# The last batch's token mixing as seven half products instead of eight, in a kernel whose matmul engine is always busy

## The chip, the cores and the metric

One core of a Trainium2 chip. The metric is the device time of one execution in microseconds (us), median of several. All data are float32. Engines: TensorE (PE, with its weight loads as PEld), VectorE (DVE), ScalarE (ACT), GpSimd (POOL), SyncE (SP, which issues all transfers).

## What is computed

Linear attention gives x, and a gated network with token mixing follows. Four batches, 1088 tokens, d_model 128, d_ff 1024; the mixing matrix is 1088 x 1088.

```python
def _moe_ref(x, w_in, w_spatial, b_spatial, w_out):
    h = np.maximum(x @ w_in, 0.0)
    u, v = h[..., :d_ff // 2], h[..., d_ff // 2:]
    v_n = (v - mean(v)) / np.sqrt(var(v) + 1e-06)          # over the 512 features
    v_s = np.einsum('ts,bsd->btd', w_spatial, v_n) + b_spatial[None, :, None]
    return (u * v_s) @ w_out
```

The product of `w_spatial` with `v_n` is the mixing; it is the largest part of the work.

## The kernel before

Every float32 operand of a matmul is kept as a high part, which the matmul takes exactly, and a low part (the rest); one product is three matmuls: high by high, low by high, high by low. `wTh` and `wTl` hold `w_spatial` transposed in SBUF for the whole kernel: 9 tiles of 128 source tokens (`kt`; the ninth holds the last 64 with the bias) by 1088 target tokens.

For each batch, `attention` makes x and then v (normalised on DVE), and `main` does the mixing. It runs over four blocks `d` of 128 features and three column groups `c` of target tokens (`CH`: 424, 332, 332 wide). For each of the 12 blocks, `hidden` makes u (three matmuls into PSUM bank `pu`, ReLU on ACT), `spatial` the mixing in one of two PSUM banks `sp`: for `kt` 0 to 7 three matmuls (L1018, L1020, L1027) and two for the ninth tile (L1018, L1029), 26 in all. `gate` then multiplies the bank by u on DVE (L1054), ACT casts the result to its high part (L525), DVE subtracts for the low part (L456), and `out_mm` adds its product with `w_out` (L446 to L448) to one of three `po` banks. A bank `sp` can be written anew only after the DVE's gate has read it. Line 936 and its neighbours split v into `vh` and `vl` for the next block.

What is executed when is not the order of the code: `Order.schedule` arranges the recorded operations on each engine from hand-set tables (`LEADS`, `T_MAIN`, `PACE`). Each engine then works strictly in the order it was given. Attention of the next batch is interleaved with the mixing of this one; in the last batch there is no next attention, and from about 260 us on PE has mixing, `hidden` and `out_mm` alone.

## Time and profile before

| | |
|---|---|
| time, median of 3 runs (lowest, highest) | 326.54 us (326.52, 327.94) |
| profiled execution, from first to last instruction | 325.6 us |
| PE busy | 319.2 us, 98% |
| DVE busy | 199.9 us, 61% |
| ACT busy | 150.9 us, 46% |
| POOL busy | 47.0 us, 14% |
| granted TensorE clock | 1.000 of full speed, 2.4 GHz, throughout |

The page states the span, 325.6 us, and no separate time for the profiled execution; the median lies 0.9 us above the span, which is taken as what lies around it. In the rows, DVE, ACT, POOL and PE are busy times of instructions; matmuls overlap, so a matmul's own duration (0.31 us) says less than the distance from one start to the next. A bracket at a row's end names the idle time before it and what ended it.

### The profile page before, as it was taken

The numbers are of one execution on the slowest core, as the hardware profiler recorded it, in microseconds if no ns is written. First come the engines' busy times: TensorE is split into PE (matmuls) and PEld (weight loads), VectorE is DVE, ScalarE is ACT, GpSimd is POOL, SyncE is SP. The second block draws the span as 40 slices with busy tenths as digits, with TensorE's granted clock in tenths as the row PEclk, the third lists the DMA queues.
The fourth block names the chain that finished last, engine by engine and source line by source line (L and its number), as shares of the span: only waits on it lengthen the run. The fifth ranks groups of instructions, "written<-read, shape, count | busy, mean of one in ns | idle before, by whom it ended". The sixth has DMA issues, their size and how long they took to land.

```text
span 325.6 us, 6652 instructions
## 1 busy us (share of the span) xinstructions
PE 319.2 (98%) x2655; PEld 303.7 (93%) x2655; DVE 199.9 (61%) x439; ACT 150.9 (46%) x357; POOL 47.0 (14%) x59
## 2 busy tenths in 40 slices
PE   8999999999999999999999999999999999999996
PEld 7877899999999899989999989999999999999995
DVE  4999899354599982679985899873222341022122
ACT  3389666634676464357542875642232242112211
POOL 1000001667300004350002812100000000000000
PEclk9999999999999999999999999999999999999999
DMA  6941059764011252310114410000000000000002
GB/s 206 337 146 49 22 148 300 231 193 128 0 48 44 84 162 89 117 34 24 45 45 129 142 50 21 0 2 0 2 0 1 29 21 23 0 0 2 0 0 70
DMA packets 18961, 23.97 MB, mean 74 GB/s; under 512 B 2546, under 2 KB 18674, under 8 KB 18930
## 3 DMA queue, kind: packets, MB, share of 16 engines
q1 hardware_dynamic: 18930, 23.54, 23.4%
q8 instruction: 21, 0.34, 0.4%
q14 instruction: 10, 0.08, 0.1%
HBM read 20.46 MB, written 3.06 MB: 72 GB/s over the span
## 4 chain that ended last, share of the span: by engine, by line
PE 83%; DMA 6%; SPq 3%; ACT 2%; POOL 2%; issue 2%; DVE 1%; POOLq 0%; ACTq 0%
PE sp L1018 18%; PE sp L1027 17%; PE sp L1020 16%; PE sd L446 3%; PE sd L447 3%; PE sd L448 3%; DMA pl<-abd 3%; PE po L446 2%; PE po L447 2%; PE po L448 2%; PE pu L446 2%; PE sp L1029 2%; PE pu L447 2%; PE pu L448 2%; DMA v<-in_vA 2%
## 5 line engine op out<-in xcount | busy, mean ns | idle before, releaser
L1018 PE MATMUL sp<-wT,vh 128*128 128x332 f32 (+1 forms) x414 | 133.8, 323 | 0.0
L1020 PE MATMUL sp<-wT,vl 128*128 128x332 f32 (+1 forms) x368 | 119.1, 324 | 0.3 <-DVE vl L965 0.3
L1027 PE MATMUL sp<-wT,vh 128*128 128x332 f32 (+1 forms) x368 | 116.9, 322 | 0.0
L1018 PEld LDWEIGHTS sp<-wT,vh 128*128 128x128 f32 x414 | 77.8, 188 | 1.9 <-ACT vh L962 0.3
L1020 PEld LDWEIGHTS sp<-wT,vl 128*128 128x128 f32 x368 | 69.1, 188 | 1.8 <-DVE vl L965 1.1
L1027 PEld LDWEIGHTS sp<-wT,vh 128*128 128x128 f32 x368 | 69.0, 188 | 0.4 <-DVE wT L573 0.2
L1054 DVE TENSOR_TENSOR u<-sp,u 128x332 f32<-128x332 f32 (+1 forms) x40 | 20.7, 517 | 51.7 <-PE sp L1029 42.7
L1010 ACT ACTIVATE u<-pu 128x332 f32<-128x332 f32 (+1 forms) x40 | 18.5, 463 | 36.9 <-PE pu L448 21.0
L456 DVE TENSOR_TENSOR g<-u,g 128x332 fp32r<-128x332 f32 (+1 forms) x38 | 21.8, 575 | 22.3 <-PE po L447 15.1
L525 ACT CAST g<-u 128x332 fp32r<-128x332 f32 (+1 forms) x38 | 18.1, 484 | 28.2 <-DVE u L1054 19.1
L874 DVE BATCH_NORM_STATS2 st<-vt 128x6 f32<-128x512 f32 x36 | 24.4, 688 | 8.2 <-ACT vt L872 7.9
L872 ACT ACTIVATE vt<-sd 128x512 f32<-128x512 f32 x36 | 21.7, 607 | 10.3 <-PE sd L448 9.5
L852 DVE RECIPROCAL c<-c 128x384 f32<-128x384 f32 (+1 forms) x9 | 21.8, 2418 | 6.7 <-ACT c L850 6.7
L791 POOL TENSOR_TENSOR pl<-pl,pl 128x384 f32<-128x384 f32 (+1 forms) x18 | 17.8, 1004 | 49.8 <-DMA pl<-abd 48.3
L934 ACT CAST vh<-vt 128x384 fp32r<-128x384 f32 x36 | 17.5, 513 | 11.6 <-PE sp L1018 6.8
L459 POOL TENSOR_TENSOR r<-pl,r 128x384 fp32r<-128x384 f32 (+1 forms) x18 | 17.3, 972 | 20.9 <-ACT r L525 15.4
L936 DVE TENSOR_TENSOR vl<-vt,vh 128x384 fp32r<-128x384 f32 (+1 forms) x36 | 19.2, 542 | 1.2 <-ACT vh L934 0.9
L573 POOL TENSOR_TENSOR wT<-pl,wT 128x332 fp32r<-128x332 f32 (+1 forms) x9 | 8.4, 956 | 56.7 <-ACT wT L570 55.0
L894 DVE TENSOR_SCALAR vt<-vt,mv,sm 128x512 f32<-128x512 f32 x33 | 16.3, 538 | 0.0
L446 PE MATMUL pu<-x,wih 128*128 128x332 f32 (+1 forms) x48 | 16.1, 335 | 0.0
L570 ACT CAST wT<-pl 128x332 fp32r<-128x332 f32 (+1 forms) x27 | 12.8, 503 | 6.7 <-DMA pl<-in_wT 6.7
L447 PE MATMUL pu<-x,wih 128*128 128x332 f32 (+1 forms) x48 | 15.7, 327 | 0.0
(153 smaller groups left out, 497.8 us busy)
## 6 DMA issues: line engine op xcount, KB each, us to landing
pl<-in_wT SPq DMA_DIRECT2D x18, 166.0 KB
v<-in_vA SPq DMA_DIRECT2D x12, 198.0 KB
kt<-in_kT SPq DMA_DIRECT2D x12, 192.0 KB
pl<-abd SPq DMA_DIRECT2D x12, 192.0 KB
pl<-abd SPq DMA_DIRECT2D x24, 96.0 KB
pl<-in_wT SPq DMA_DIRECT2D x9, 212.0 KB
c<-in_qT SPq DMA_DIRECT2D x7, 192.0 KB
out<-u SPq DMA_DIRECT2D x6, 166.0 KB
```

The costliest lines, as they stand in the source:

```text
L446: nc.tensor.matmul(o, ah, bh, start=start, stop=False)
L447: nc.tensor.matmul(o, ah, bl, start=False, stop=False)
L448: nc.tensor.matmul(o, al, bh, start=False, stop=stop)
L456: return lambda: nc.vector.tensor_tensor(out=o(), in0=a(), in1=bb(), op=ALU.subtract)
L852: op("DVE", 135 + 6.3 * n, lambda x32=x32, n=n: nc.vector.reciprocal(out=x32[:, :n], in_=x32[:, :n]), w=[x32])
L872: op("ACT", c_act(512, True) + 16, lambda pv=pv, t=t: nc.scalar.activation(vt[:, t], pv.ap, AF.Relu), r=[pv], w=[(vt, t)])
L874: op("DVE", 690, lambda stats=stats, t=t: nc.vector.bn_stats(out=stats.ap, in_=vt[:, t]), r=[(vt, t)], w=[stats])
L936: return lambda: eng.tensor_tensor(out=vl[:, kk:kk + n], in0=x()[:, :n], in1=vh[:, kk:kk + n].bitcast(F32), op=ALU.subtract)
L1018: nc.tensor.matmul(sp[:, :cw], vh[:, kt], wTh[:, kt, cs], start=(kt == 0), stop=False)
L1020: nc.tensor.matmul(sp[:, :cw], vl[:, kt], wTh[:, kt, cs], start=False, stop=False)
L1027: nc.tensor.matmul(sp[:, :cw], vh[:, kt], wTl[:, kt, cs], start=False, stop=False)
L1054: op("DVE", c_dve(cw), lambda: nc.vector.tensor_tensor(out=u.ap, in0=sp[:, :cw], in1=u.ap, op=ALU.mult), r=[sp], w=[u], lead=LEAD[1])
```

## The change

In batch 3 (`FAST`), `main_fast` takes the place of `main`. The first eight tiles of source tokens are cut into two halves of four, the target tokens into two halves of 552 columns (268 + 284; twelve columns between 756 and 768 of the padded matrix are a gap of zeros), and the feature blocks go in pairs (d, e). This makes a 2 x 2 by 2 x 2 block product, which Winograd's form of Strassen's method does with seven block products instead of eight, of sums of blocks. The ninth tile (`remainder`) stays apart.

- `weights_fast` loads 48 pieces of `w_spatial` again from HBM (128 x 268 or 284, 4 buffers `w`, issued after 185 us in the schedule's time), forms the sums S1, S2, S4 and S3 from them on DVE (72 operations) and splits them into high (32 casts on ACT) and low parts. They are written where attention's buffers lie, S3 over columns of `wT`.
- `prepare(p)` forms the sums of blocks of v for a pair.
- `product` does one block product (4 tiles x 3 matmuls for each of the two column pieces). What several results share is kept: `keep` copies a bank to SBUF on ACT, and `gate` with `other` first adds it (L1424) and then multiplies (L1434).
- `out_mm` adds up one pair at a time; the first pair's result is kept by an ACT copy, the second pair's added on DVE (L1472), and four stores leave instead of three.
- `CH`, `AT` and `PITCH` change the order and place of the column groups, and the tables of the schedule are new for batches 2 and 3.

```diff
-CH = [(0, 424), (424, 332), (756, 332)]
-AT = [0, 436, 820]
+CH = [(332, 424), (0, 332), (756, 332)]
+AT = [332, 0, 768]
+CW = (268, 284)
+FROM = ((0, 268), (548, 816))
+FAST = (3,)
+RELOAD = 185.0
+USE_POOL = False
-T_MAIN = (36.0, 126.0, 244.0, 299.0)
-PACE = (1.305, 0.8, 1.056, 1.506)
+T_MAIN = (36.0, 126.0, 222.612, 333.931)
+PACE = (1.305, 0.8, 1.0625, 1.8734)
...
+        def block(kt, half, c):
+            t = tl("w", f"wr{kt}{half}{c}", [P, CW[1]])
+            load(t, lambda: t[:, :CW[c]], wT[kt * P:(kt + 1) * P, c0:c0 + CW[c]], CW[c] // 2, after=RELOAD)
...
+        def halves(j, i, c, x):
+            op("ACT", c_act(n), lambda: nc.scalar.copy(out=hi(), in_=x[:, :n]), r=[x], w=wh)
+            both(c_dve(n), tt(lo, lambda: x[:, :n], lambda: hi().bitcast(F32), ALU.subtract), [x, *wh], wl, c_pool(n))
+        for i in range(4):
+            for c in range(2):
+                a21, a22 = block(i, 1, c), block(4 + i, 1, c)
+                sum_of(a22, a21, a22, ALU.add, c)
+                halves(1, i, c, a22)
...
+            a11, a12 = block(i, 0, c), block(4 + i, 0, c)
+            both(c_dve(n), tt(lambda: a11[:, :n], lambda: hi().bitcast(F32), lambda: a11[:, :n], ALU.subtract), wh, [a11], c_pool(n))
+            both(c_dve(n), tt(lambda: a11[:, :n], lambda: a11[:, :n], lambda: lo().bitcast(F32), ALU.add), wl, [a11], c_pool(n))
+            halves(2, i, c, a11)
+            sum_of(a12, a12, a11, ALU.subtract, c)
+            halves(4, i, c, a12)
...
+                a11, a21 = block(i, 0, c), block(i, 1, c)
+                sum_of(a11, a11, a21, ALU.subtract, c)
+                halves(3, i, c, a11)
...
+        def product(q, w, bank, c, start):
+            for i in range(4):
+                    nc.tensor.matmul(o, s, ap(i, 0, c), start=start and not i, stop=False, skip_group_check=not start)
+                    nc.tensor.matmul(o, l, ap(i, 0, c), start=False, stop=False, skip_group_check=not start)
+                    nc.tensor.matmul(o, s, ap(i, 1, c), start=False, stop=i == 3, skip_group_check=not start)
...
+        for p in range(2):
+            for c in range(2):
+                product(q, a11, cs[c], c, True)
+                x1.append(keep("x1", p, c, cs[c]))
+            for c in range(2):
+                product(q + 1, a12, ys[c], c, True)
+                edge_of(ys[c], c, 0, d)
+                gate(d, 0, c, ys[c], u[c], x1[c])
+            for c in range(2):
+                product(q + 2, block_s(1), xs[c], c, True)
+                p5.append(keep("p5", p, c, xs[c]))
+            for c in range(2):
+                product(q + 3, block_s(4), xs[c], c, False)
+                edge_of(xs[c], c, 0, e)
+                mix.append(keep("mx", p, c, xs[c]))
+            for c in range(2):
+                product(q + 4, block_s(2), cs[c], c, False)
+                gate(e, 0, c, cs[c], u[c], mix[c])
+            for c in range(2):
+                product(q + 5, block_s(3), cs[c], c, False)
+                edge_of(cs[c], c, 1, e)
+                gate(e, 1, c, cs[c], u2[c], p5[c])
+            for c in range(2):
+                product(q + 6, a22, cs[c], c, False)
...
+                gate(d, 1, c, cs[c], u[c])
```

The new lines of old code: L1018 is L1088, L1020 is L1090, L1027 is L1097, L1029 is L1099, L446 to L448 are L511 to L513, the gate L1054 is L1124. DVE's sums and low parts of the change all carry L1185, the products' matmuls L1359 to L1361, those of the ninth tile L1371 and L1372, those of `out_mm` in batch 3 L1448 to L1450. `sp`, `sd`, `pu` and `po` with a number are PSUM banks; `w_...` are the buffers of reloaded pieces, `later_...`, `area_...` and `wi_...` places of their sums.

On each engine the order is the one before for the first 911 of PE's instructions (to about 126 us) and for DVE to about 120 us; from there the two differ. The first place is in batch 2, on VectorE, around the gate of the second block of 424 columns. Before, DVE has there the end of the normalisation of batch 3's v and then the gate:

```order
L880 RECIPROCAL sm_520<-sm_508 128x3
L885 SCALAR_TENSOR_TENSOR sm_513<-mv_487,sm_520 128x3
L885 SCALAR_TENSOR_TENSOR sm_513<-sm_513,sm_520 128x3
L885 SCALAR_TENSOR_TENSOR sm_520<-sm_513,sm_520 128x3
L885 SCALAR_TENSOR_TENSOR sm_537<-mv_487,sm_520 128x3
L894 TENSOR_SCALAR vt_148<-vt_148,mv_487,sm_520 128x512 x3
L1054 TENSOR_TENSOR u_199<-sp_295,u_199 128x424
L936 TENSOR_TENSOR vl<-vt_148,vh 128x2x128
```

After the change, sums of `w_spatial` stand between these:

```order
L957 SCALAR_TENSOR_TENSOR small<-small 128x3
L1185 TENSOR_TENSOR vt<-vt 128x4x128
L957 SCALAR_TENSOR_TENSOR small<-small 128x3
L966 TENSOR_SCALAR vt<-vt,small 128x512 x3
L1185 TENSOR_TENSOR w_2258<-w_2279,w_2258 128x284
L1185 TENSOR_TENSOR w_2272<-later_2352,w_2272 128x268
L1185 TENSOR_TENSOR vh<-vt,vh 64x128
L1185 TENSOR_TENSOR w_2272<-w_2272,later_2352 128x268
L1124 TENSOR_TENSOR u_200<-sp_288,u_200 128x424
L1185 TENSOR_TENSOR w_2266<-w_2266,w_2272 128x268
```

Between the normalisation and the gate there are now three sums (L1185 on `w_...`) and one low part of v's ninth tile. On PE, before, this block of 424 columns (bank `sp_295`) is followed by `hidden` and by fifteen matmuls of a block of 332 columns in the other bank, of which two are shown; then `sp_295` is written again:

```order
L1018 MATMUL sp_295<-wT,vh 128x424
L1029 MATMUL sp_295<-wT,v_99 128x424
L446 MATMUL pu_185<-x,wih_67 128x332
L447 MATMUL pu_185<-x,wih_67 128x332
L448 MATMUL pu_185<-x,wil_71 128x332
L1018 MATMUL sp_273<-wT,vh 128x332
L1020 MATMUL sp_273<-wT,vl 128x332
```

after the change six matmuls in the other bank follow, and then the bank of that gate is written again:

```order
L1088 MATMUL sp_288<-wT,vh 128x424
L1099 MATMUL sp_288<-wT,v_116 128x424
L1088 MATMUL sp_268<-wT,vh 128x332
L1090 MATMUL sp_268<-wT,vl 128x332
L1097 MATMUL sp_268<-wT,vh 128x332
L1088 MATMUL sp_268<-wT,vh 128x332
L1090 MATMUL sp_268<-wT,vl 128x332
L1097 MATMUL sp_268<-wT,vh 128x332
L1088 MATMUL sp_288<-wT,vh 128x332
L1090 MATMUL sp_288<-wT,vl 128x332
```

What moved: the bank comes back after 6 matmuls instead of 18.

The second place is in batch 3, on PE. Before, the shortest return to a bank there is this, at the end of a block in `sp_273`, with three matmuls of `out_mm` and three of the other bank between:

```order
L1029 MATMUL sp_273<-wT,v_97 128x332
L446 MATMUL po_152<-g,woh 128x332
L447 MATMUL po_152<-g,woh 128x332
L448 MATMUL po_152<-g,wol 128x332
L1018 MATMUL sp_295<-wT,vh 128x332
L1020 MATMUL sp_295<-wT,vl 128x332
L1027 MATMUL sp_295<-wT,vh 128x332
L1018 MATMUL sp_273<-wT,vh 128x424
```

After the change, the fifth product of the first pair (q + 4, from S2) ends in `sd_132`, and the sixth (q + 5, from S3, which lies in `wT`) adds to the same bank after the gate's addition has read it:

```order
L1361 MATMUL sd_132<-x,vh 128x268
L1359 MATMUL sd_99<-wT,vh 128x284
L1360 MATMUL sd_99<-wT,vl 128x284
L1361 MATMUL sd_99<-wT,vh 128x284
L1359 MATMUL sd_99<-wT,vh 128x284
L1360 MATMUL sd_99<-wT,vl 128x284
L1361 MATMUL sd_99<-wT,vh 128x284
L1359 MATMUL sd_132<-wT,vh 128x268
```

Six matmuls stand between in both; those of the change are narrower.

## Rows read from the trace of the kernel before

**Rows 1.** The page's head, busy time of each engine with its share of the span and its instructions, and the chain of work that ended last.

```profile
span 325.6 us, 6652 instructions
PE 319.2 (98%) x2655; PEld 303.7 (93%) x2655; DVE 199.9 (61%) x439; ACT 150.9 (46%) x357; POOL 47.0 (14%) x59
...
PE 83%; DMA 6%; SPq 3%; ACT 2%; POOL 2%; issue 2%; DVE 1%; POOLq 0%; ACTq 0%
```

**Rows 2.** Busy time of each engine in five stretches (from:to, length, then PE, PEld, DVE, ACT, POOL, each with its instructions, the granted TensorE clock, the DMA share and GB/s).

```profile
180.00:188.00 8.00, 8.00 (x55) 7.99 (x53) 7.35 (x8) 5.78 (x14) 6.73 (x8) 1.00 0.36 113
188.00:210.00 22.00, 21.98 (x125) 20.30 (x124) 19.90 (x45) 14.58 (x34) 2.51 (x3) 1.00 0.07 26
210.00:222.00 12.00, 12.00 (x70) 11.53 (x69) 8.79 (x24) 5.05 (x12) 1.41 (x2) 1.00 0.01 1
222.00:240.00 18.00, 18.00 (x115) 17.96 (x114) 5.25 (x11) 5.02 (x12) 0.00 (x0) 1.00 0.00 1
...
258.00:280.00 22.00, 22.00 (x137) 21.95 (x136) 5.28 (x11) 5.80 (x14) 0.00 (x0) 1.00 0.07 24
...
```

**Rows 3.** What DVE waited for, and what PE waited for (us in total, times, longest us).

```profile
DVE u L1054 <- PE sp L1029: 42.7, 17, 5.5
...
PE sd L469 <- DVE z L465: 1.3, 1, 1.3
...
```

**Rows 4.** The timeline of PE in a stretch of mixing matmuls of 332 columns in batch 3: the first row, and the row twelve matmuls later (start, duration, engine, line, operation, tiles, shape).

```profile
313.94 0.31 PE L1018 MATMUL sp<-wT,vh 128*128 128x332 f32 x1
...
315.70 0.31 PE L1018 MATMUL sp<-wT,vh 128*128 128x332 f32 x1
```

**Rows 5.** The same for 424 columns: the first row, and the row eight matmuls later.

```profile
243.04 0.35 PE L1020 MATMUL sp<-wT,vl 128*128 128x424 f32 x1
...
244.53 0.35 PE L1018 MATMUL sp<-wT,vh 128*128 128x424 f32 x1
```

**Rows 6.** The timeline of PE at two calls of `hidden`, which read x: 424 columns (three matmuls and the first behind them), then 332 columns.

```profile
240.57 0.35 PE L446 MATMUL pu<-x,wih 128*128 128x424 f32 x1
...
241.15 0.36 PE L1018 MATMUL sp<-wT,vh 128*128 128x424 f32 x1
...
246.60 0.31 PE L446 MATMUL pu<-x,wih 128*128 128x332 f32 x1
...
247.06 0.32 PE L1018 MATMUL sp<-wT,vh 128*128 128x332 f32 x1
```

**Rows 7.** The timeline of PE's weight loads where twelve follow each other with the kernel's narrow attention matmuls.

```profile
22.71 1.42 PEld L738 LDWEIGHTS sp<-abT,c 128*128 128x128 f32 x12 [0.23 <-issue]
...
```

**Rows 8.** Groups of VectorE's and ScalarE's instructions by line and shape (count, busy us, mean ns, idle time before them).

```profile
L456 DVE TENSOR_TENSOR g<-u,g 128x332 fp32r<-128x332 f32 x30 | 17.1, 572 | 21.1 <-PE po L447 14.2 <-ACT g L525 6.9
...
L965 DVE TENSOR_TENSOR vl<-vt,vh 128x512 fp32r<-128x512 f32 x8 | 5.4, 679 | 0.4 <-ACT vh L962 0.4
L525 ACT CAST g<-u 128x332 fp32r<-128x332 f32 x30 | 13.9, 467 | 20.7 <-DVE u L1054 19.1 <-PE po L448 1.4
```

**Rows 9.** The timeline of DVE: a gate with the instruction behind it.

```profile
251.11 0.51 DVE L1054 TENSOR_TENSOR u<-sp,u 128x332 f32<-128x332 f32 x1 [3.80 <-PE sp L1029]
251.53 0.89 DVE L936 TENSOR_TENSOR vl<-vt,vh 128x384 fp32r<-128x384 f32 x2
```

**Rows 10.** The timeline of DVE and POOL where both work, and of DVE shortly after with POOL idle; in brackets, what ended the engine's idle time.

```profile
187.91 0.87 POOL L791 TENSOR_TENSOR pl<-pl,pl 128x320 f32<-128x320 f32 x1 [0.62 <-DMA pl<-abd]
...
187.95 1.25 DVE L853 TENSOR_TENSOR c<-c,c 128x384 f32<-128x384 f32 x1
189.12 0.55 DVE L936 TENSOR_TENSOR vl<-vt,vh 128x384 fp32r<-128x384 f32 x1
...
210.16 1.41 POOL L859 CAST x<-x 128x64 fp32r<-128x64 f32 x2 [11.24 <-DVE x L456]
```

**Rows 11.** The timeline of SP's queue: the last two loads of `abd` for attention 3, the second of which releases POOL at 187.91 in the group above.

```profile
184.46 1.20 SPq L790 DMA_DIRECT2D pl<-abd  x2
```

**Rows 12.** The timeline of PE and DVE around the second block of 424 columns in batch 2: its last matmul, the next matmul into the same bank; on DVE the normalisation's last three instructions and the gate.

```profile
218.37 0.35 PE L1029 MATMUL sp<-wT,v 66*128 66x424 f32 x1
...
221.22 0.31 PE L1018 MATMUL sp<-wT,vh 128*128 128x332 f32 x1
...
218.37 1.45 DVE L894 TENSOR_SCALAR vt<-vt,mv,sm 128x512 f32<-128x512 f32 x3
219.74 0.59 DVE L1054 TENSOR_TENSOR u<-sp,u 128x424 f32<-128x424 f32 x1
```

**Rows 13.** The timeline of PE and DVE at a block's end in batch 3: the last matmul into the bank, its gate, the next matmul into the same bank.

```profile
300.81 0.31 PE L1029 MATMUL sp<-wT,v 66*128 66x332 f32 x1
...
301.86 0.36 PE L1018 MATMUL sp<-wT,vh 128*128 128x424 f32 x1
...
301.16 0.50 DVE L1054 TENSOR_TENSOR u<-sp,u 128x332 f32<-128x332 f32 x1 [2.42 <-PE sp L1029]
```

**Rows 14.** The timeline of the tail: PE's last mixing matmul, the gate behind it, its low part (the cast lies between), PE's last matmul.

```profile
319.68 0.31 PE L1029 MATMUL sp<-wT,v 66*128 66x332 f32 x1
...
320.03 0.50 DVE L1054 TENSOR_TENSOR u<-sp,u 128x332 f32<-128x332 f32 x1 [2.23 <-PE sp L1029]
...
321.13 0.50 DVE L456 TENSOR_TENSOR r<-u,r 128x332 fp32r<-128x332 f32 x1 [0.18 <-ACT r L525]
...
322.09 0.31 PE L448 MATMUL po<-r,wol 128*128 128x332 f32 x1
```

More of the change, by code (lines that the diff above doesn't have):

```diff
@@ L371, in c_mm, with cols, toks @@
     return k * C_MM[cls or n] if (cls or n) in C_MM else k * max((n + 11.8) / 2.25, 111)
+def cols(kt, c0, cw):
+    return frozenset((kt, s) for s, (a, e) in enumerate(zip(SEGS, SEGS[1:])) if a < c0 + cw and e > c0)
+def toks(t, ds=range(ND)):
+    return frozenset((t, d, x) for d in ds for x in range(2))
 @with_exitstack
@@ L405, in tile_kernel @@
     homes |= {(t, i): homes["x"][:, n, i] for n, t in enumerate(("xh", "xl")) for i in range(SB_BUFS[t])}
+    early = {"kt": 384, "v": 396, "kp": 768}
+    middle = {"c": 384, "abT": 192, "pl": 424}
+    extra = {"r": 384, "kvh": 256, "kvl": 256}
+    parts = (early, middle, extra)
+    sizes = [sum(n * Order.bufs(t) for t, n in part.items()) for part in parts]
+    areas = [const.tile([P, n], F32R if j == 2 else F32, name=f"area{j}", tag=f"area{j}", bufs=1) for j, n in enumerate(sizes)]
+    spans, again = [], {2: areas[2]}
@@ new lines, in tile_kernel, with later @@
+    for j, (area, part) in enumerate(zip(areas, parts)):
+        end = 0
+        for tag, n in part.items():
+            m = Order.bufs(tag)
+            homes[tag] = area[:, end:end + m * n].rearrange("p (n c) -> p n c", n=m)
+            homes |= {(tag, i): homes[tag][:, i] for i in range(m)}
+            spans += [(j, end + i * n, end + i * n + n, tag) for i in range(m)]
+            end += m * n
+    def later(j):
+        if j not in again:
+            again[j] = const.tile([P, sizes[j]], F32R, name=f"later{j}", tag=f"area{j}", bufs=1)
+        return again[j]
@@ L407, in place @@
+    homes["vd0", 0] = flat[:, 4 * CW[1]:4 * CW[1] + P]
+    small = const.tile([P, 6 * SB_BUFS["st"] + 6 * SB_BUFS["mv"] + 3 * SB_BUFS["sm"]], F32, name="small")
+    end = 0
+    for tag, n in (("st", 6), ("mv", 6), ("sm", 3)):
+        homes |= {(tag, i): small[:, end + i * n:end + i * n + n] for i in range(SB_BUFS[tag])}
+        end += n * SB_BUFS[tag]
     def place(t):
+        if t.tag == "ge":
+            return later(0)[:, t.slot * CW[1]:(t.slot + 1) * CW[1]]
         if t.name in ("wTh", "wTl"):
@@ L897, in act @@
                 nc.scalar.activation(vt[:, t], vt[:, t], AF.Identity, bias=nm[:, t:t + 1], scale=rs[:, t:t + 1])
-            op("DVE", c_dve2(DH, True), dve, r=[mv, rs, nm], w=[(vt, t)], sh=True, alts=[("ACT", c_act(DH, ptr=True), act)], kind=f"norm{b}")
+            op("DVE", c_dve2(DH, True), dve, r=[mv, rs, nm], w=[(vt, toks(t))], sh=True, alts=[("ACT", c_act(DH, ptr=True), act)], kind=f"norm{b}")
     def main(b, st):
         po = [None] * 3
-        wide = b == B - 1
-        cols = CH
         def big(c):
-            return c == 0 and (wide or not b)
+            return c == 0 and not b
         clock, rate = [T_MAIN[b] * 1e3], [1.0]
@@ L965, in low @@
                     return lambda: eng.tensor_tensor(out=all_d(ls), in0=x(), in1=all_d(hs).bitcast(F32), op=ALU.subtract)
-                op("DVE", c_dve(DH), low(nc.vector), r=[(vt, t), *((h, kt) for h in hs)], w=[(l, kt) for l in ls], sh=True, alts=[("POOL", c_pool(DH), low(nc.gpsimd))], kind="vl0")
+                op("DVE", c_dve(DH), low(nc.vector), r=[(vt, toks(t)), *((h, kt) for h in hs)], w=[(l, kt) for l in ls], sh=True, alts=[("POOL", c_pool(DH), low(nc.gpsimd))], kind="vl0")
             else:
@@ L996, in store @@
                     op("SP", 470, lambda: nc.sync.dma_start(out=out[b, :, c0 + at:c0 + at + n], in_=ob[:, at:at + n]), r=r, kb=n // 2, due=late, lead=-12000)
[L999 removed]
+                copy("ACT", 0, cw, 0)
                 store(0, cw, [ob])
         def hidden(d, c, tag="pu"):
[L1003 removed]
+            c0, cw = CH[c]
             pu = bank(tag, f"pu{b}{d}{c}")
```

346 lines of the change are left out of this document (311 added, 35 removed).

## The prediction, made before the changed kernel ran

> **What bounds the kernel now.** First the page's head and its chain [rows 1]: PE is busy 98% of a span of 325.6 us, and 83% of the chain that ended last is PE; no other engine has more than 2% of it but the start's transfers. Next the stretches [rows 2]: from 188 us on PE is busy for the whole of each, at the full clock (granted 1.00, its level of 2.4 GHz), so neither its clock nor a wait is to be won there; only fewer or shorter matmuls are. The waits say the same from the other side [rows 3]: DVE waits 42.7 us for the last matmul of a block, in 17 waits, while the longest wait of PE is 1.3 us. So the end is set by PE's work, as long as the others keep up. Who could fall behind is also in [rows 2]: DVE is busy 7.35 of 8 us from 180, 19.90 of 22 us from 188 and 8.79 of 12 us from 210 (attention 3 and its normalisation), and only about a quarter to a third from 222 on. POOL is nearly done by 212. DMA is almost idle from 188 on (share 0.07 and less).
>
> A matmul's price is a distance between starts. On `wT`, twelve matmuls of 332 columns take 315.70 - 313.94 = 1.76 us, 0.1467 each [rows 4]; eight of 424 take 1.49 us, 0.186 each [rows 5]. That is 0.430 ns for each column and some 4 ns besides. On x, in `hidden`, 424 columns take 0.58 / 3 = 0.193 us and 332 take 0.46 / 3 = 0.153 [rows 6], about 6.5 ns more each.
>
> **PE's work in batch 3.** Before, 12 blocks of 26 mixing matmuls: 104 of 424 columns at 0.186 and 208 of 332 at 0.1467, 19.4 + 30.5 = 49.9 us. `hidden` and `out_mm` have 24 of 424 and 48 of 332, at the price on x 4.6 + 7.3 = 12.0. Together 61.9 us, which is what the program has from 260 us to the last matmul. After: 7 products x 4 tiles x 3 matmuls x 2 pieces x 2 pairs = 336, and 32 of the ninth tile; half are 268 wide, half 284. By 0.430 ns a column they cost 0.1192 and 0.1261: 184 x 0.1192 + 184 x 0.1261 = 45.1 us. `hidden` and `out_mm` become 96 of 268 (24), 284 (48) and 252 (24) columns at the price on x, 0.125, 0.132 and 0.118: 12.2. Some pieces start elsewhere in their tile than `wT`'s columns did, 0.2 us. Together 57.5. PE is relieved of 61.9 - 57.5 = 4.4 us; I take **4.3**. The ends: 4.7 if all matmuls run at the price on `wT`, 2.0 if all 368 cost the 6.5 ns that x does (2.4 us). I take a value near the upper end because the nearest rows, `wT` itself, are where two of the three operands of most products lie.
>
> Each matmul needs a new weight load, which must now fit 0.119 us. Twelve loads in a row take 1.42 us, 0.118 each, with their narrow matmuls [rows 7]: they just fit. If the pace were 0.13 the products would cost 2.8 us more and 1.6 us of the gain be left.
>
> Batches 0 to 2 keep their matmuls and column widths, so there is nothing for PE there, by count.
>
> **VectorE's added work.** A gate of 332 columns leaves DVE free after 251.53 - 251.11 = 0.42 us, though it is listed with 0.51 [rows 9]; between that and 512 columns (0.679 [rows 8]) a column costs about 1.0 ns, so a sum of 276 columns takes some 0.36 us from start to start. The 72 operations of the two waves are 26 us, the 32 casts of ACT, at 0.47 for 332 columns [rows 8], 13 us; ACT has room for these throughout. Of DVE's 72, the changed order has 17 ahead of the gate of batch 2's second block of 424 columns (near 220 us), 47 between that and the last gate of batch 2 (near 258), the rest in batch 3.
>
> From 188 to 222 DVE has 34.0 - 19.9 - 8.8 = 5.3 us idle [rows 2], and gets 17 x 0.36 = 6.1. That is 0.8 too much, just where the second 424 block ends. There the trace shows how little is to spare [rows 12]: the block's last matmul starts at 218.37, DVE is then in the normalisation for 1.4 us, and the gate runs from 219.74 to 220.33; PE came back to the bank at 221.22, 2.85 us behind that matmul. In the changed order it comes back after six matmuls, 0.19 + 6 x 0.1467 = 1.07 us behind it. With a gate as late as before (1.96 us from the matmul to its end) PE would wait 0.9 us; with a gate at once, none. I take **+0.8**, bounds 0 and 2.2 (the three sums that now stand between normalisation and gate, 1.1 us, and v's ninth tile, 0.3, on top). What waits with the gate: DVE's next sums, and of PE everything, since it works in order. From 222 to 258 DVE has some 24 us idle by [rows 2] (busy 5.25 of 18 us and much the same after), and gets 47 x 0.36 = 17: enough on the whole, so this is one stall and not a chain of them.
>
> **Hand-offs in batch 3.** Before, the tightest return to a bank is in [rows 13]: last matmul at 300.81, gate 301.16 to 301.66, bank used again at 301.86, without a wait. So a bank costs 0.35 + 0.50 = 0.85 us, and had 1.05. In the changed order six matmuls lie between (second place in the order): 0.12 + 6 x 0.126 = 0.88 us, against 0.35 + 0.43 for 268 columns. It fits by 0.1 us if DVE is free at that moment. DVE was busy 5.28 of 22 us there [rows 2]; with the sums of blocks of v, the additions ahead of the gates and the rest of S3 this about doubles, so it mostly is. At the end, the last gate to the end of its low part took 319.68 to 321.63 [rows 14]; the changed order has 14 narrower matmuls (1.8 us) in that time, 0.1 to 0.3 short. For four or five such places I take **+0.6**, bounds 0 and 3.
>
> **The sum** is made on the span: 325.6 - 4.3 + 0.8 + 0.6 = 322.7; with the 0.9 us that the median of 326.5 lies above the span, **323.6 us**.
>
> **Rivals.** A difference of 0.5%, 1.6 us, is about what a measurement of this kernel can tell from no change: faster is below 324.9, slower above 328.2.
>
> *Full gain.* Nothing waits: the gates find DVE idle and hand-offs fit. For it: each fits by itself. Against: the 0.8 too much. 326.5 - 4.3 (or 4.7) = 321.8 to 322.2. Chance 0.10.
>
> *Dear half products.* The narrower matmuls cost the price on x, or the weight load's: gain 1.6 to 2.0, so 326.5 - 1.8 + 1.4 = 326.1. For it: 0.119 is hardly above 0.118 [rows 7]; sums lie in tiles placed elsewhere. Chance 0.11.
>
> *Hand-offs everywhere.* There are 28 products in banks that are read and written again. If each lost 0.12 us, that is 3.4 instead of 0.6: 326.4. Against: most have far more than six matmuls between. Chance 0.08.
>
> *POOL in DVE's way.* At 187.95 DVE's operation with two operands in SBUF took 1.25 us beside POOL's at 187.91, while the same shape took 0.55 at 189.12 with POOL idle [rows 10]. The sums are of this kind. POOL still has five operations between 188 and 222 [rows 2]; if each met a sum, 5 x 0.7 = 3.5 us would be added to DVE's lateness at the gate: 323.6 + 2.5 (a third falls into idle time) = 326.1. Against: the sums are a fifth of DVE's time there. Chance 0.06. The Trainium skill, "SBUF — State Buffer", section "Who interferes with whom", says that a VectorE instruction with two SBUF inputs contends with a GpSimd instruction that reads SBUF, and that the second to issue is blocked until the first is done. By that rule, the trace agrees: 1.25 is about 0.87 and the rest of the shape's 0.55.
>
> *Loads too slow, the side of slower.* The sums take their pieces through four buffers, so two pairs of the 24 are under way at once, and a sum whose piece has not come holds DVE and every gate behind it. Two loads issued at 184.46 were there at 187.91, 3.45 us [rows 10, 11]. A pair is then held for 1.3 us (sum, cast, low part) in the waves of S1 and S3 and 2.8 us in that of S2 (five DVE operations, two casts): 8 rounds x 4.75 + 4 x 6.25 = 63 us, 188 to 251, while PE needs S3 near 279. That fits. But from 222 to 258 DVE has only 24 - 17 = 7 us over, with some seven rounds in it: each us on top of 3.45 costs all gates 7 us in sum, less the first 7 of slack. It decides when more than 5.3 us of lateness reach PE (4.3 - 0.6 + 1.6), which is at a load of about 5.2 us; at 5.5 us it is 14 - 7 = 7 us late and 330. For it: the loads are 134 to 142 KB each, and reading them again is 6.6 MB in the busiest part of DVE. Against: the queues are empty there. Chance 0.13.
>
> **Numbers.** The forecast's own case, 322.4 to 324.9, has 0.52. Faster: 0.52 + 0.10 = 0.62; same: 0.11 + 0.08 + 0.06 = 0.25; slower: 0.13. The range from 322.0 to 326.4 leaves out the slow case and a few of the others, not quite 2 in 10.
>
> The Trainium skill, "TensorE: Matmul & The Clock Gate", section "LDWEIGHTS (loading the stationary operand)", gives a load of 128 columns as 128 / 1.2 = 107 ns; by it the half products would have 12 ns to spare and *dear half products* would fall to the placement alone. The row above (0.118 with what surrounds it) neither shows nor excludes this.
>
> **What would show it.** In the changed profile: products at 0.119 and 0.126 from start to start (*dear*: 0.125 to 0.13); PE with one idle stretch of about 0.8 us at the return to the bank of the second 424 block, and none above 0.5 in batch 3; DVE busy over 95% from 188 to 222 and about 80% to 258, with hardly any idle time put down to a transfer (*loads*: several waits of over 1 us for `w` pieces, and PE waiting for gates behind them); no sum of over 0.6 us after 200 (*POOL*). The prediction is wrong if PE's batch 3 is not near 57.5 us of work, or if PE waits for more than 3 us between 188 and its last matmul.

## The result, and the profile after

The changed kernel takes 329.36 us (median of 7 runs, 328.96 to 330.92); the kernel before, run beside it, 327.51 us (7 runs). The ratio is 1.0068, 95% interval 1.0047 to 1.009: slower by 0.7%, where 323.6 us had been forecast. (The 326.54 us of the table above is the median of the first three of those seven.) The profiled execution's span is 327.9 us.

The head of the page after and its chain, against [rows 1]:

```profile
span 327.9 us, 7140 instructions
PE 320.5 (98%) x2735; PEld 303.5 (93%) x2735; DVE 241.7 (74%) x552; ACT 173.9 (53%) x421; POOL 48.3 (15%) x61
...
PE 78%; DVE 10%; DMA 5%; ACT 4%; issue 2%; SPq 0%; DVEq 0%; ACTq 0%
```

PE is still the bound, and it is busy for 1.3 us longer, although its work by columns has become less. Busy times of the engines by stretch after the change (columns as in [rows 2]):

```profile
188.00:210.00 22.00, 21.66 (x125) 20.11 (x124) 20.93 (x47) 15.82 (x38) 4.06 (x4) 1.00 0.26 80
210.00:222.00 12.00, 12.00 (x67) 11.38 (x66) 11.98 (x35) 6.29 (x14) 0.93 (x2) 1.00 0.31 84
222.00:240.00 18.00, 17.94 (x108) 17.37 (x107) 16.58 (x40) 8.85 (x22) 0.00 (x0) 1.00 0.28 74
258.00:280.00 22.00, 22.00 (x169) 21.98 (x168) 15.16 (x34) 12.64 (x33) 0.00 (x0) 1.00 0.30 86
```

DVE is busy 97% from 188 to 222 us, as forecast (over 95%), and 92% to 240, and PE hardly waits for it (busy 21.66 of 22 us, then nearly all). The clock is granted in full (1.00, the 2.4 GHz level). So the time isn't lost in waits of that kind. It is in the distance from one matmul to the next. The timeline of PE after the change, first and last row each: a run of 29 matmuls of 424 columns, of 78 of 332 columns (both in batch 2), of 12 matmuls of a half product of 268 columns and of 15 of 284:

```profile
230.05 0.36 PE L511 MATMUL po<-g,woh 128*128 128x424 f32 x1
...
235.49 0.35 PE L1099 MATMUL sp<-wT,v 66*128 66x424 f32 x1
...
249.54 0.31 PE L1088 MATMUL sp<-wT,vh 128*128 128x332 f32 x1
...
261.18 0.32 PE L1099 MATMUL sp<-wT,v 66*128 66x332 f32 x1
...
273.20 0.28 PE L1359 MATMUL sp<-later,vh 128*128 128x268 f32 x1
...
274.56 0.29 PE L1361 MATMUL sp<-wi,vh 128*128 128x268 f32 x1
...
319.26 0.29 PE L1360 MATMUL sd<-wT,vl 128*128 128x284 f32 x1
...
321.09 0.29 PE L1371 MATMUL sd<-wT,g 128*128 128x284 f32 x1
```

424 columns: 5.44 us / 28 = 0.194 us, 0.186 in [rows 5]. 332 columns: 11.64 / 77 = 0.1512, 0.1467 in [rows 4]. 268: 1.36 / 11 = 0.1236 (forecast 0.1192). 284: 1.83 / 14 = 0.1307 (forecast 0.1261). The matmuls of batches 0 to 2, which the change doesn't touch, have become 4.5 to 8 ns dearer each in these rows.

**Where the 2.3 us of span come from.** I went through PE's starts in both traces and split each distance into three: the matmul's columns by 0.4427 ns (near what [rows 4, 5] give in their long runs: 332 x 0.4427 = 147 ns), an excess of up to 18 ns above that, and, above 18 ns, a stall. For matmuls of 200 columns and more:

| us | before | after |
|---|---|---|
| columns, change | | -5.1 |
| excess, batches 0 to 2 (to 260.5 us) | 2.9 | 6.2 |
| excess, batch 3 | 0.4 | 2.3 |
| stalls, batches 0 to 2 | 6.5 | 5.5 |
| stalls, batch 3 | 0.0 | 2.2 |
| PE's last matmul starts at | 322.09 | 323.66 |
| from there to the end | 3.5 | 4.2 |

The excess grows by 5.2 us and by itself eats the whole gain of 5.1. It is not the new order: up to 126 us, where PE's instructions have the order of before, it already grows from 1.2 to 2.6 us.

In the kernel before, a matmul of 332 columns takes 152.0 ns right after a change of width (mean of the first three of a run) and then comes down: 150.0 from the fourth to the sixth, 149.1 from the seventh to the twelfth, 147.7 from the thirteenth on; 424 columns go from 192.8 over 191.0 and 188.2 to 187.5. I call that settling. After the change the figures for 332 are 151.3, 151.5, 151.2 and 151.4: nothing settles.

### The profile page after: what moved, and what is told of

It is laid out like the page before. It is cut to its first block, busy times and chain, and to the rows that moved or that the text cites. A ratio compares the mean times of both kernels' runs of the same rounds, so it can differ in the third digit from the quotient of the medians.

```text
span 327.9 us, 7140 instructions
## 1 busy us (share of the span) xinstructions
PE 320.5 (98%) x2735; PEld 303.5 (93%) x2735; DVE 241.7 (74%) x552; ACT 173.9 (53%) x421; POOL 48.3 (15%) x61
## 4 chain that ended last, share of the span: by engine, by line
PE 78%; DVE 10%; DMA 5%; ACT 4%; issue 2%; SPq 0%; DVEq 0%; ACTq 0%
PE sp L1088 13%; PE sp L1097 12%; PE sp L1090 11%; PE sd L1359 3%; PE sd L1360 2%; PE sd L1361 2%; PE sd L511 2%; PE sd L512 2%; PE sd L513 2%; PE pu L511 2%; PE pu L513 2%; PE pu L512 2%; PE sp L1359 2%; PE sp L1361 2%; PE sp L1360 2%; DMA vt<-in_w_in 2%
## 5 line engine op out<-in xcount | busy, mean ns | idle before, releaser
L1088 PE MATMUL sp<-wT,vh 128*128 128x332 f32 (+1 forms) x306 | 100.1, 327 | 0.1
L1090 PE MATMUL sp<-wT,vl 128*128 128x332 f32 (+1 forms) x272 | 88.8, 326 | 0.3 <-DVE vl L1035 0.3
L1097 PE MATMUL sp<-wT,vh 128*128 128x332 f32 (+1 forms) x272 | 87.0, 326 | 0.0
L1088 PEld LDWEIGHTS sp<-wT,vh 128*128 128x128 f32 x306 | 57.5, 188 | 2.3 <-issue 0.6
L1090 PEld LDWEIGHTS sp<-wT,vl 128*128 128x128 f32 x272 | 51.1, 188 | 1.9 <-DVE vl L1035 0.9
L1097 PEld LDWEIGHTS sp<-wT,vh 128*128 128x128 f32 x272 | 51.1, 188 | 0.6
L946 DVE BATCH_NORM_STATS2 small<-vt 128x6 f32<-128x512 f32 x36 | 24.5, 690 | 6.7 <-ACT vt L944 6.3
L924 DVE RECIPROCAL area<-area 128x384 f32<-128x384 f32 (+1 forms) x9 | 21.8, 2418 | 10.2 <-ACT area L922 10.0
L1124 DVE TENSOR_TENSOR u<-sp,u 128x332 f32<-128x332 f32 (+1 forms) x32 | 16.5, 518 | 12.2 <-PE sp L1099 7.9
L863 POOL TENSOR_TENSOR area<-area 128x384 f32<-128x384 f32 (+1 forms) x18 | 17.9, 1007 | 46.9 <-DMA area<-abd 42.5
L524 POOL TENSOR_TENSOR area<-area,area 128x384 fp32r<-128x384 f32 (+1 forms) x18 | 17.7, 986 | 20.7 <-ACT area L590 14.6
L511 PE MATMUL pu<-x,wih 128*128 128x332 f32 (+4 forms) x52 | 17.0, 328 | 0.3 <-ACT u L1080 0.3
L966 DVE TENSOR_SCALAR vt<-vt,small 128x512 f32<-128x512 f32 x33 | 16.6, 535 | 0.0
L513 PE MATMUL pu<-x,wil 128*128 128x332 f32 (+4 forms) x52 | 16.4, 315 | 0.0
L512 PE MATMUL pu<-x,wih 128*128 128x332 f32 (+4 forms) x52 | 16.4, 315 | 0.0
```

The lines of the kernel that those rows point to most:

```text
L511: nc.tensor.matmul(o, ah, bh, start=start, stop=False)
L512: nc.tensor.matmul(o, ah, bl, start=False, stop=False)
L513: nc.tensor.matmul(o, al, bh, start=False, stop=stop)
L524: return lambda: nc.gpsimd.tensor_tensor(out=o(), in0=a(), in1=bb(), op=ALU.subtract)
L863: op("POOL", c_pool(n), lambda fa=fa, fb=fb: nc.gpsimd.tensor_tensor(out=fa[:, :n], in0=fa[:, :n], in1=fb[:, :n], op=ALU.mult), r=[fb], w= ...
L924: op("DVE", 135 + 6.3 * n, lambda x32=x32, n=n: nc.vector.reciprocal(out=x32[:, :n], in_=x32[:, :n]), w=[x32])
```

## Experiments

The first suspect was the layout. The change narrows the rows of `wTh` and `wTl` in SBUF (the rows of W from here on) from 1152 to 1120 elements:

```diff
-PITCH, G_PITCH, G_AT = 1152, 448, {424: 0, 332: 52}
+PITCH, G_PITCH, G_AT = 1120, 448, {424: 0, 332: 52}
```

**e1 and e2: the row pitch alone, in the kernel before.** e1 takes 1120 elements (4480 B, with the third piece at column 772 as there is no room at 820), e2 1184 (4736 B). The order of all instructions is that of the kernel before.

> The kernel before with two numbers changed: the row pitch of wT 1120 instead of 1152 elements (the value of the changed kernel; 4480 bytes instead of 4608), and the third column group at 772 instead of 820 so that it fits. Order of every engine, columns and matmuls are those of before. Theory A (the row pitch decides the rhythm of the matmuls on wT: in the changed kernel 332 columns went from 147 to 152 ns and 424 from 187 to 194 ns in all batches): the same two changes show here, about 1250 mixing matmuls times 4 to 6 ns, so 327.5 + 5 to 7 = 332 to 334 us. Rival B (something else in the changed kernel, its new traffic of ACT, DVE and transfers or the shifted start of the tile, slows the matmuls): 147 and 187 ns stay and the time is that of before, 327.5 within 0.5 us.

> The kernel before with one number changed: the row pitch of wT 1184 instead of 1152 elements, 4736 bytes, wider rather than narrower, column groups where they were. Theory A in its form 'only a pitch of a whole number of 512 bytes keeps the rhythm': slowed as with 1120, 332 to 334 us, 332 columns at about 151 ns. Its other form 'a narrower pitch or the moved third group is to blame': 147 ns and 327.5. Rival B: 327.5.

e1: 331.35 us, ratio 1.0111 (1.0068 to 1.0155); e2: 330.95 us, 1.0112 (1.0082 to 1.0143). In both, 332 columns take 152 ns and 424 take 194 (medians; 147 and 187 before), and the excess is 8.6 and 8.3 us instead of 3.3. The layout alone costs 3.7 and 3.3 us, without a single half product.

**e3: the distance between `wTh` and `wTl`,** in the changed kernel 128 B more, so that it is the same within 512 B as before.

```diff
-            at = NS * PITCH * (t.name == "wTl")
+            at = (NS * PITCH + 32) * (t.name == "wTl")
```

> The changed kernel with 32 elements between the high and the low half of wT, so that they lie 40448 bytes apart (a whole number of 512) instead of 40320; the row pitch stays 1120. If the distance of the two halves alone sets the rhythm, two of three steps between matmuls become as before and the time falls by 3 to 5 us, to 324.5 to 326.5; if the row pitch sets it, as theory A has it, nothing moves: 329.4 within 0.6 us and 332 columns stay at 152 ns.

329.46 us, ratio 1.004 (1.0007 to 1.0073); 152 and 193 ns, excess 8.2 us. It isn't that distance.

**e4: 66 rows instead of 64.** The stalls of batch 3 stand at four places. PE's timeline of the changed kernel at the first:

```profile
289.98 0.29 PE L1371 MATMUL sd<-wT,g 128*128 128x284 f32 x1
290.20 0.39 PE L1372 MATMUL sd<-wT,wi 64*128 64x284 f32 x1
290.52 0.40 PE L1359 MATMUL sp<-wT,vh 128*128 128x284 f32 x1
290.76 0.29 PE L1360 MATMUL sp<-wT,vl 128*128 128x284 f32 x1
```

Around the one matmul with 64 rows the distances are 0.22, 0.32 and 0.24 us, where neighbours have 0.13: 0.4 us for each of the four. The other products with the ninth tile have 66 rows (64 and the two bias rows) and no such gap. e4 gives these four two rows of zeros.

```diff
-                remainder(cs[c], c, 1, ..., [vds[p][1]], 64)
+                remainder(cs[c], c, 1, ..., [vds[p][1]], 66)
...
+            op("DVE", 120, lambda: nc.vector.tensor_tensor(out=vd[1][64:66], in0=z9[64:66], in1=z9[64:66], op=ALU.subtract), r=[z9], w=[vd[1]])
```

> The changed kernel with one thing undone: in the last product's part of the ninth tile the second matmul takes 66 rows instead of 64, as the kernel before does everywhere, with two rows of zeros written by two small DVE operations. In the profile each of the four places where a matmul of 64 rows stands among those of 128 loses about 0.1 us before it, 0.2 behind it and 0.1 behind the next. Theory C (the change of the number of rows costs it): the four triples vanish, 4 x 0.4 = 1.6 us, 327.8. Rival (these are waits for a bank or for a weight load that happen to lie there): 329.4 within 0.5 us, and the triples stay.

328.26 us, ratio 1.0004 (0.9985 to 1.0024), 1.1 us less than the changed kernel and 1.2 less than e3 of the same set of runs. PE's timeline at the same place, without a gap:

```profile
289.69 0.29 PE L1371 MATMUL sd<-wT,g 128*128 128x284 f32 x1
289.82 0.30 PE L1372 MATMUL sd<-wT,wi 66*128 66x284 f32 x1
289.95 0.30 PE L1359 MATMUL sp<-wT,vh 128*128 128x284 f32 x1
290.09 0.29 PE L1360 MATMUL sp<-wT,vl 128*128 128x284 f32 x1
```

Stalls in batch 3 fall from 2.2 to 0.7 us. The Trainium skill, "TensorEngine Tiling (Array Packing)", section "Available Configurations", lists 64 rows as a tiling of its own beside the full 128. That fits the shape of the loss; the section gives no time for going from one to the other, and the runs show 0.4 us for one such matmul in between. That the loss is such a switch isn't shown; that it comes with the 64 rows is.

**e5 to e8: other pitches, in the kernel before.** e5 is e1 with an unused tile behind the rows, so that all tiles behind them lie where they lay; e6 to e8 have rows of 1104, 1136 and 1128 elements.

```diff
+    const.tile([P, 2 * NS * 32], F32, name="rest")        # e5, behind wT
-PITCH = 1152
+PITCH = 1120   (e5), 1104 (e6), 1136 (e7), 1128 (e8)
```

> The kernel before with rows of W of 1120 elements (4480 B), as in the earlier run with that pitch, but with an unused tile of 2304 B put behind the rows, so that every tile behind them lies where it lay before. If the row pitch itself takes the rhythm away: the 332 column matmuls on W stay at 152 ns and the 424 column ones at 194 ns from start to start, and the time is about 331 us. If it is the place of the other tiles (g, x, the areas that VectorE, ScalarE and the DMAs write), the matmuls are back at 147 and 187 ns and the time at 327.5 us.

> The kernel before with rows of W of 1104 elements (4416 B, an odd multiple of 64 B). If only a row pitch that is a multiple of 512 B lets the matmuls fall into the rhythm: 152 and 194 ns, about 331 us. If the two slow pitches so far (4480 and 4736 B) are slow because they are multiples of 128 B but not of 256, or because of some narrower relation between rows, this one may be fast: 147 and 187 ns, 327.5 us. I hold the first for likelier, 7 in 10.

> The kernel before with rows of W of 1136 elements (4544 B, another odd multiple of 64 B, but 64 B from 4608 where 4416 is 192 B from it). Same alternatives: 152 and 194 ns and about 331 us if only multiples of 512 B are fast; 147 and 187 ns and 327.5 us if odd multiples of 64 B do as well.

> The kernel before with rows of W of 1128 elements (4512 B, no multiple of 64 B, so that the columns of a piece begin at another place within 64 B in every second row). If only multiples of 512 B are fast: 152 and 194 ns, about 331 us. If what counts is that the same columns begin at the same place in each 64 B, this one is slower than the other pitches; if the alternation itself carries the rhythm, faster.

331.57, 331.44, 331.99 and 331.12 us (two runs each; ratios 1.0133, 1.0129, 1.0146, 1.0119, all intervals above 1), with 152 and 193 to 194 ns in all four. The place of the other tiles is not it, and of six pitches in all only 4608 B settles. At this point I held the theory that the pitch has to be a multiple of 512 B.

**e9 and e10: the changed kernel with the pitch of before.** For room, `ka` and the zeros for the warm-up lie in the buffers of the W loads, g directly behind the last row, and the split bias in two row ends. e10 has the 66 rows too.

```diff
-PITCH, G_PITCH, G_AT = 1120, 448, {424: 0, 332: 52}
+PITCH, G_PITCH, G_AT = 1152, 448, {424: 0, 332: 52}
```

> The changed kernel with the row pitch of W back at 1152 elements (4608 B), the columns of the change (with their gap of 12), its order on every engine and its arithmetic unchanged. Room for the longer rows: three small buffers of the early batches lie in the buffers of the W loads, g behind the last row, the split bias in the unused end of a row. If the row pitch is the cause of the loss: 332 columns at 147 ns, 424 at 187, 268 at about 119 and 284 at about 126 from start to start, the time above 17/16 cycles a column down from 8.4 us to about 3.2, and the kernel at 329.4 - 5.2 = 324.2 us, 1% below the kernel before. If the half products can't keep the rhythm whatever the pitch: 332 and 424 as said, but 268 and 284 still at 124 and 131 ns, and 326.1 us, as only 3.3 of the 5.25 us stand ahead of 260 us. If the loss comes from other parts of the change: 152 and 194 ns as now, 329.4 us.

> The same, and the four matmuls of 64 rows made 66 rows long with two rows of zeros (as in the earlier run with 66 rows, which took 1.1 us off). If the two losses are apart from each other: 324.2 - 1.1 to 1.6 = 322.6 to 323.1 us, 1.4% below the kernel before. If the stalls at those four places were only hidden waits that come back elsewhere once PE runs faster: 324.2 us.

e9: 328.30 us, ratio 1.0024 (1.0005 to 1.0042). e10: 326.78 us, 0.9971 (0.9952 to 0.9989). Only part came back, and in a pattern that the theory doesn't give: 424 columns settle as before (189 ns, median 187), 332 only in part (150, median 151), the half products not at all (124 and 131). The excess of e9 is 6.2 us, not 3.2. The 66 rows again are worth 1.5 us.

**e11 and e12: the place within 512 B, and the length of a run.** e11 is e10 with one 64 B buffer moved from ahead of the rows of W to behind them; the column pieces then start at the same bytes within 512 as before. e12 adds that a product's twelve matmuls are one step of the schedule (second diff).

```diff
-    homes["rec", 1] = const.tile([P, 3 * H], F32, name="rec1")     # ahead of wT
+    homes["rec", 1] = const.tile([P, 3 * H], F32, name="rec1")     # behind it
```

```diff
-                op("PE", c_mm(n, 3), f, r=[(hs[d], h), (ls[d], h), *r(i, c)], ...)      # for each of four tiles
+            op("PE", c_mm(n, 12), f, r=[(hs[d], h), (ls[d], h), *(x for i in range(4) for x in r(i, c))], ...)
```

> The kernel of the run before (row pitch 4608 B, 66 rows), with one 64 B buffer put behind the rows of W instead of ahead of them, so that the column pieces begin at the same place within 512 B as in the kernel before (240, 240 and 32 B, where they began at 304, 304 and 96 B). With the pitch back, the 424 column matmuls settle as they did before the change (187 ns), but the 332 ones only in part (mean 149.4 to 150.9 ns by stretch, 148.4 before the change). If the place within 512 B is what is left of that: 332 columns at 147 to 148.5 ns in the first three batches, about 600 matmuls by 1.7 ns = 1.0 us less than 326.8, 325.8 us. If what is left comes from the order, which changes widths in other places than before: no change, 326.8 us. I hold them for equally likely. The half products (268 and 284 columns) stay at 124 and 131 ns by both.

> The same kernel, but each half product's twelve matmuls are one step of the planner, so that no matmul of another width stands between them; before they stand in runs of 3 to 12. In the kernel before a 332 column matmul needs 3.2 ns more than 17/16 cycles a column right after a change of width, 1.6 at the fifth and 0.3 from the seventh on. If the half products cost 124 and 131 ns only because their runs are too short to settle: the later ones of a run of twelve come down towards 119 and 126 ns. If they are slow by their width or the places of their rows: 124 and 131 ns at all positions of the run. The time may rise by either, since steps of twelve leave the planner less to choose from; only the matmul times are read.

e11: 328.61 us, ratio 1.0036 (1.0016 to 1.0056). By neither expectation: 64 B cost 1.8 us against e10 (of another set of runs), and now nothing settles, 424 columns neither (194 ns), although the pitch is 4608 B. So the pitch by itself can't be the cause, nor the place of W's rows. e12, 329.21 us, says nothing on its question, since nothing settles in it. What had changed between e10 and e11 is the distance of W's rows from `vh` and `vl`, the weights that PE loads while it reads these rows. One weight tile lies at `vh` + 2048 B x `kt` + 512 B x slot. With rows of 4608 B (9 x 512) the distance between row and weights, within 512 B, is the same for every `kt`; with 4480 B it changes by 128 B from one `kt` to the next.

**e13 to e16: the distance.** e13 is the kernel before with 64 unused bytes between the weights and W, so that W and all tiles behind it move, e14 with the same 64 bytes ahead of everything. e15 is e10 with small buffers moved so that W's distances from both `vh` and `vl` are those of before (g's rows become 432 elements for room). e16 is e15 with products in one step.

```diff
+    const.tile([P, 16], F32, name="gap64")     # e13: ahead of wT; e14: ahead of ka0, the first tile
```

```diff
     weights("vh", "wih0", "woh")
+    small = const.tile(...)                    # e15: 384 B between vh and vl, from behind vt
     weights("vl", "wil0", "wol")
+    bh, bl = const.tile([P, 16], F32R) ...     # e15: 128 B between vl and wT
```

> The kernel before, pitch 4608 B, with an unused 64 B between the stationary operands (vh, vl) and the rows of W: every row of W and all behind it lies 64 B further, vh and vl stay. Distances of a piece's start from vh within 512 B: 0, 208, 208 in place of 448, 144, 144. If the distance between moving and stationary operand carries the rhythm: 332 columns at 152 ns and 424 at 194 ns, or part of the way there, and 330 to 331.5 us. If the pitch alone carries it: 147 and 187 ns, 327.5 us.

> The kernel before with the same unused 64 B ahead of all its buffers, so that vh, vl and W move together and every distance between them is kept. If the distance carries the rhythm: 147 and 187 ns, 327.5 us. If the absolute place of W does (its starts are those of the run before, 96, 304 and 304 B within 512 B): as the run before.

> The changed kernel with pitch 4608 B and 66 rows (326.8 us), with small buffers placed so that the rows of W stand to both vh and vl as in the kernel before, within 512 B (448, 144, 144 and 64, 272, 272 B; in the run of 326.8 us only the distance to vh was that of before, the one to vl was 448, 144, 144). If the distances carry the rhythm: 332 columns at 148 to 148.5 ns by stretch (150 there), excess in the first three batches from 3.8 to about 2.9 us, 325.8 us. If not: 326.8 us or, as in the run with W moved by 64 B, 328.6 us.

> The same with each half product's twelve matmuls in one run. If the half products on the rows of W (the quarters of W that are read there, four of seven products) are slow by the shortness of their runs: from the seventh of a run on they take 119 to 121 ns (268 columns) and 126 to 128 (284), while those on x and the other areas, whose rows stand at changing distances from the stationary operand, stay at 124 and 131. If they are slow by their width: 124 and 131 ns at all positions.

e13: 332.51 us, ratio 1.0146 (1.0092 to 1.02). e14: 327.52 us, 1.0011 (0.9979 to 1.0043). e15: 326.12 us, 0.9969 (0.9943 to 0.9996). e16: 327.69 us, 1.001 (0.9983 to 1.0036). The last 84 matmuls of 332 columns that follow each other in batch 3, first and last row on PE's timeline, in the kernel before:

```profile
307.86 0.31 PE L446 MATMUL pu<-x,wih 128*128 128x332 f32 x1
...
320.13 0.32 PE L448 MATMUL po<-g,wol 128*128 128x332 f32 x1
```

in e14, where all moved by 64 B:

```profile
307.86 0.32 PE L446 MATMUL pu<-x,wih 128*128 128x332 f32 x1
...
320.14 0.32 PE L448 MATMUL po<-g,wol 128*128 128x332 f32 x1
```

and in e13, where W moved and the weights did not:

```profile
311.81 0.32 PE L446 MATMUL pu<-x,wih 128*128 128x332 f32 x1
...
324.45 0.32 PE L448 MATMUL po<-g,wol 128*128 128x332 f32 x1
```

12.27, 12.28 and 12.64 us: 0.1478, 0.1480 and 0.1523 for each. All kernels side by side, the distances in bytes within 512 for the piece of 424 columns and the two of 332 (for `kt` 0 where they change), and the mean distance of starts from the thirteenth matmul of a run on:

| kernel | to `vh` | to `vl` | 332, ns | 424, ns |
|---|---|---|---|---|
| before | 448, 144, 144 | 64, 272, 272 | 147.7 | 187.5 |
| e14 | 448, 144, 144 | 64, 272, 272 | 147.8 | 187.7 |
| e13 | 0, 208, 208 | 128, 336, 336 | 152.1 | 192.6 |
| after | 320, 16, 16, changing | 448, 144, 144, changing | 151.4 | 193.6 |
| e10 | 448, 144, 144 | 448, 144, 144 | 150.2 | 189.0 |
| e11 | 384, 80, 80 | 384, 80, 80 | 151.6 | 194.1 |
| e15 | 448, 144, 144 | 64, 272, 272 | 148.4 | 188.8 |

Where both distances are those of before, the matmuls settle; where only the one to `vh` is (e10), 424 columns settle as far as in e15 (189.0 and 188.8 ns) and 332 in part; else nothing does. In e1 the pieces at columns 0 and 436 have the distances of before within 128 B at every `kt`, and yet nothing settles, so the relation reaches over more than 128 B. Which distances are good beyond the one pair seen, and why, wasn't tried.

The same runs as above in e15, 29 matmuls of 424 and 78 of 332 columns:

```profile
228.30 0.36 PE L511 MATMUL po<-wT,woh 128*128 128x424 f32 x1
...
233.59 0.35 PE L1099 MATMUL sp<-wT,v 66*128 66x424 f32 x1
...
247.40 0.32 PE L1088 MATMUL sp<-wT,vh 128*128 128x332 f32 x1
...
258.82 0.31 PE L1099 MATMUL sp<-wT,v 66*128 66x332 f32 x1
```

5.29 us and 11.42 us, where the changed kernel has 5.44 and 11.64. The half products are another matter. In e16 they stand in runs of twelve. Only the pieces of 268 columns that begin at W's column 0, as one piece of 332 does, have that piece's distances of 144 and 272 B; the other pieces on W lie at 192 to 352 B from `vh`. PE's timeline, one of three such runs at column 0:

```profile
283.56 0.29 PE L1359 MATMUL sp<-wT,vh 128*128 128x268 f32 x1
...
284.92 0.29 PE L1361 MATMUL sp<-wT,vh 128*128 128x268 f32 x1
```

1.36 / 11 = 0.1236 us, as in the changed kernel; the other two have 0.1232 and 0.1234. In the same kernel 332 columns have come down from 151.7 to 149.1 ns by the seventh to the twelfth of a run. Over all pieces, by place in the run, 268 columns take 123.8 (first to third), 123.5, 123.7 and 124.3 ns (thirteenth on); 284 take 131.5, 131.5, 130.9 and 131.3. So for 268 columns, twelve in a row at distances at which 332 settle are not enough. That they settle later or never is what is left there; the pieces of 284 may need other distances as well. The runs don't tell which.

e15 has the lowest time of all: 1.2 us below the kernel before, with an interval that just excludes no change. From e10, of another set of runs, its time can't be told apart (ratios 0.9969 and 0.9971); what e15 shows is the distance of starts, and the excess ahead of batch 3, which goes from 4.1 us in e10 to 3.3.

## Why the prediction was wrong

**The step that failed** is the sentence "Batches 0 to 2 keep their matmuls and column widths, so there is nothing for PE there, by count". The count is right and the price isn't. The change moves the rows of W in SBUF, `PITCH` stood in the diff, and with it moved the distance to the weights on which the 147 and 187 ns of [rows 4, 5] rest. That cost 3.3 us in batches 0 to 2: the excess there is 6.2 us instead of 2.9. e1 and e2 show the loss without the rest of the change, e13 with 64 B alone, and in e15, the changed kernel with the distances of before, that excess is down to 3.3 us. No rival had it; the chance of 0.13 for slower was that of another mechanism.

**The price of the half products** was mis-sized: 0.1236 and 0.1307 us, not 0.1192 and 0.1261. I took the settled price of other widths for them and argued from where their operands lie. The dearer price that [rows 6] show was read as that of x; but both calls stand right behind a change of width, and `wT` costs as much there. PE's timeline of the kernel before, behind the second call:

```profile
247.06 0.32 PE L1018 MATMUL sp<-wT,vh 128*128 128x332 f32 x1
...
247.37 0.31 PE L1027 MATMUL sp<-wT,vh 128*128 128x332 f32 x1
```

Two starts on `wT` in 0.31 us, 0.155 each, against 0.153 on x. So batch 3's relief is 5.1 of columns less 1.9 of excess, 3.2 us, not 4.3. That is inside the bounds (2.0 to 4.7). The rival *dear half products* had the price (0.125 to 0.13) nearly right, and at 2.4 us the loss too high: the 368 matmuls cost 1.7 more than forecast. The cost tables of the schedule, which the prediction doesn't use, had both: `C_MM` of the changed kernel plans with 122.5 and 128.0 ns for these widths, and `SETTLE` of both kernels adds 32.2 ns to the first fourteen matmuls of 332 columns in a run.

**From span to time,** the sum adds 0.9 us, the median of 326.5 less the span of 325.6. These two belong to different executions. Wherever the record has time and span of the same run, the time is 1.7 to 2.0 us longer (329.65 and 327.9 for the changed kernel's profile), so this term was 0.9 too small. On the span itself 322.7 had been forecast and 327.9 measured, 5.2 more: 3.3 of excess in batches 0 to 2, 1.1 of batch 3's relief, 0.7 of the tail, 0.2 of narrow matmuls, less 0.1, as the stalls grew by 1.3 us where 0.8 + 0.6 had been added.

**VectorE's lateness** was forecast at 0.8 us at the return to the bank of the second 424 block. The place is right. PE's timeline there, with DVE's gate (before: [rows 12]):

```profile
223.47 0.35 PE L1099 MATMUL sp<-wT,v 66*128 66x424 f32 x1
...
224.41 0.31 PE L1097 MATMUL sp<-wT,vh 128*128 128x332 f32 x1
224.79 0.42 PE L1088 MATMUL sp<-wT,vh 128*128 128x332 f32 x1
...
224.14 0.59 DVE L1124 TENSOR_TENSOR u<-sp,u 128x424 f32<-128x424 f32 x1
```

The block's last matmul had started at 223.47; the gate ends at 224.73 and the next matmul starts at 224.79, 0.38 us behind its predecessor, and the one after it 0.25 behind that, instead of 0.15 each: 0.33 us in all. The gate ends 1.26 us behind the block's last matmul, not 1.96 as before. Over batches 0 to 2 stalls even fell by 1.0 us; what made them fall isn't shown. DVE's sums cost 0.36 us from start to start (median), as forecast.

**Hand-offs in batch 3** were forecast at 0.6 us. Of the 2.2 us of stalls there, 1.6 are the matmuls of 64 rows, which I hadn't seen as a cost; the 0.6 to 0.7 that e4 and e10 leave are about what was meant.

**The tail** was left out of the sum: from the last matmul to the end 4.2 us instead of 3.5. The queue's row of the stores' issues, after and before:

```profile
320.57 4.41 SPq L1473 DMA_DIRECT2D out<-vt  x4
321.61 1.63 SPq L996 DMA_DIRECT2D out<-vt  x3
```

The last issue ends at 324.98, 0.54 us behind the last DVE result (324.44) and 1.3 behind the start of the last matmul; the span ends 2.9 us later. Before, the last issue ended at 323.24, 1.15 us behind the last matmul's start, and the span 2.4 later. So 0.5 of the 0.7 us lies behind the last issue. Why wasn't tried.

**Rivals.** *Loads too slow* is refuted. DVE waited for a reloaded piece once, for 0.2 us; DVE's wait:

```profile
DVE w L1185 <- DMA w<-in_wT: 0.2, 1, 0.2
```

*POOL in DVE's way* showed once, at a sum beside an operation of POOL (DVE's and POOL's timeline):

```profile
194.89 1.15 POOL L524 TENSOR_TENSOR area<-area,area 128x320 fp32r<-128x320 f32 x1 [4.86 <-ACT area L590]
195.21 1.13 DVE L1185 TENSOR_TENSOR w<-w,w 128x268 f32<-128x268 f32 x1
```

1.13 us where such a sum has 0.44; after 200 us no sum of `w_spatial` is that long. *Full gain* would have needed settled half products.

## What to carry to other kernels

A change that moves buffers is a change to every matmul that reads them: look at the addresses of both operands before and after, and take a price from the old trace only where their distance stays. For a width that the trace doesn't have, take the price of a matmul that has not settled (here 4 to 6 ns more) until a run shows better. Keep the row counts of neighbouring matmuls alike, if need be with rows of zeros.
